# Spectral filter of batches 1 to 3: the sum of two products formed by an accumulating transfer from GpSimd

## The chip, the cores and the metric

The kernel runs on one core of one Trainium2 chip. The metric is device time in microseconds (us) for one execution; the time of a kernel is the median of several runs. The engines are named as in the profile: PE is TensorE's matmul, PEld its weight load, DVE is VectorE, ACT is ScalarE, POOL is GpSimd and SP is SyncE, whose queue issues the transfers of the kernel before. L12 is line 12 of the kernel.

## The reference

Three layers follow one another on a tensor of 4 batches, 3008 tokens and 256 features, all in float32. The first is a long convolution along the tokens, written as a filter in frequency space; the other two are wide feed-forward layers. The change touches the line `Y = X * F`.

```
X = np.fft.rfft(x, axis=1)
F = (filt_r + 1j * filt_i)[None, :, :]
Y = X * F
y = np.fft.irfft(Y, n=x.shape[1], axis=1)

h = x @ w_in                 # 256 -> 2048
x = square(maximum(h, 0)) @ w_out
g = x @ w_gate               # 256 -> 1536
out = (g * sigmoid(g) * (x @ w_val)) @ w_out2
```

## The kernel before

**Arithmetic.** A float32 matrix is split into a high part (ScalarE's copy to fp32r, `high`, L353) and a low part (VectorE's subtraction, `low`, L357). A product of two such pairs is three matmuls accumulated in PSUM (`product`, L365 to L367). So nearly every operand of TensorE passes through ScalarE and then through VectorE.

**The filter.** 3008 is 64 x 47. For each batch, step A (12 groups) transforms along the 64, and its result goes to the DRAM tensor `s1`. Then 16 pairs of rows `q` are worked on one at a time. Step B loads `bin` (from `s1`) and `fil` (the filter), 192 KB each, splits `bin` into `fhi` and `flo`, multiplies by a cosine and sine matrix into the PSUM bank `psB`, and applies the filter with `filtered` (L509). That function forms the product of both components with the real part (tile `t1`, L519), two products of the swapped components with the imaginary part and a sign (tile `t2`, L524, twice), and adds `t2` into `t1` (L536). All four are VectorE operations on 96 partitions. The trace writes `t` for both tiles. `fsplit` then splits the sum into a new `fhi` and `flo`, and step C, which is called one hook later, multiplies them into `psC`, copies the bank to `eb` and stores it into `s2`. Batch 0 is filtered ahead of everything by `first_ab`, with plain float32 matmuls; it also calls `filtered`. Batches 1 to 3 go through `stages_ab`, a few steps at a time, between the matmuls of the two feed-forward layers. They are 48 steps B and 48 steps C.

**The feed-forward layers.** The tokens are cut into column pairs (`WIDTH`, up to 2 x 512), and each layer goes through its weights in groups. Most of it uses a Strassen-Winograd scheme with seven products in place of eight (`slot1`, `slot2`): a PSUM bank (`pA`, `gA`, `vA`) is copied out by ScalarE (`snap`, L955), and then more products are accumulated on top of it, so the copy has to be done before TensorE goes on with that bank. The results are split (`ghi`, `glo`) and multiplied into the banks `acc`. The weights are decoded at the start (`decode`, VectorE L428 to L450), kept in DRAM and loaded group by group by SP.

**Order of the work.** All of it is recorded as steps in a list (`Plan`). `emit` goes through the list once, before the program is built. It keeps a clock for each of the five queues, and on the queue that is free first it takes the step that can begin first; among those within 0.12 us of one another it takes the one of lowest rank, which is mostly the order of declaration. So the order of every queue is fixed beforehand by assumed costs, and on the chip each engine executes its queue in that order and waits where an input is late. An SP transfer of `kb` KB is assumed to occupy the queue for 0.55 us, and its data to be there at

```
wire = max(wire, s.end) + s.kb / 370.0
s.end = max(s.end + 2.0 + s.kb / 230.0, wire + 1.8)
```

where `s.end` is the end of the issue and `wire` a clock for the DMA engines. Tiles come from small pools of buffers: `pool_f` has 12 for the filter's tiles, and a buffer is handed on in the order of declaration when its last user is done by the plan's clock.

Of the kernel before, what the change touches and what calls it, by code (L numbers as in the profile page):

```python
# [13 lines left out]
ALU = mybir.AluOpType  # L14
# [152 lines left out]
class Plan:  # L167
# [10 lines left out]
    def add(self, engine, cost, fn, r=(), w=(), rank=0, kb=0):  # L178
        s = Step()
        s.i, s.engine, s.cost, s.fn, s.kb = len(self.steps), engine, cost, fn, kb  # L180
        s.rank, s.after, s.end, s.start = len(self.steps) + rank + self.bias, [], None, None
        deps = set()
        for key in r:
            if key in self.last:
                deps.add(self.last[key])
        for key in w:
            if key in self.last:
                deps.add(self.last[key])
            deps.update(self.readers.get(key, ()))
        deps.discard(s.i)  # L190
        for key in w:
            self.last[key] = s.i
            self.readers[key] = []
        for key in r:
            if key not in w:
                self.readers.setdefault(key, []).append(s.i)
        tiles = []
        for key in list(r) + list(w):
            t = key[0] if isinstance(key, tuple) else key
            if isinstance(t, Tile) and t not in tiles:  # L200
                tiles.append(t)
                t.users += 1
        s.deps, s.tiles = deps, tiles
        self.steps.append(s)
        return s.i

    def emit(self):
        steps = self.steps
        waits = [len(s.deps) for s in steps]
        for s in steps:  # L210
            for d in s.deps:
                steps[d].after.append(s.i)
        engines = ["PE", "ACT", "DVE", "POOL", "SP"]
        now = {e: 0.0 for e in engines}
        wire = 0.0
        open_ = {e: [] for e in engines}
        base = {}
        frontier, entered = 0, 0
        done = 0

        def enter(s):
            at = 0.0
            for d in s.deps:
                o = steps[d]
                lag = self.CROSS[s.engine] if o.engine != s.engine else 0.03
                at = max(at, o.end + lag)
            base[s.i] = at
            open_[s.engine].append(s)

        def begin(s):  # L230

            at = base[s.i]
            for t in s.tiles:
                if t.slot is None:
                    b = t.buffers
                    if not b.loose and t.turn != b.taken:
                        return None
                    best = min((b.free[k] for k in t.among), default=None)
                    if best == float("inf"):
                        return None  # L240
                    at = max(at, best + 0.15)
            return at

        while done < len(steps):
            while entered < len(steps) and entered < frontier + self.WINDOW:
                if waits[entered] == 0:
                    enter(steps[entered])
                entered += 1
            pick, when = None, None
            for e in engines:  # L250
                best = None
                ready = []
                for s in open_[e]:
                    at = begin(s)
                    if at is not None:
                        ready.append((max(at, now[e]), s))
                if not ready:
                    continue
                first = min(a for a, _ in ready)
                for a, s in ready:  # L260
                    if a <= first + (0.12 if e != "SP" else 0.0) and (best is None or s.rank < best[1].rank):
                        best = (a, s)
                if pick is None or best[0] < when:
                    when, pick = best
            assert pick is not None, "no step can begin"
            s = pick
            open_[s.engine].remove(s)
            s.start = when
            now[s.engine] = when + s.cost
            s.end = when + s.cost  # L270
            if s.engine == "SP":
                wire = max(wire, s.end) + s.kb / 370.0
                s.end = max(s.end + 2.0 + s.kb / 230.0, wire + 1.8)
            for t in s.tiles:
                if t.slot is None:
                    b = t.buffers
                    k = min(t.among, key=lambda k: b.free[k])
                    t.slot = k
                    b.taken += 1
                    b.free[k] = float("inf")  # L280
                    t.t = b.pool.tile(t.shape, t.dtype, name=t.name, tag=b.tags[k], bufs=1)
            s.fn()
            for t in s.tiles:
                t.users -= 1
                t.end = max(t.end, s.end)
                if t.users == 0:
                    t.buffers.free[t.slot] = t.end
            done += 1
            for a in s.after:
                waits[a] -= 1  # L290
                if waits[a] == 0 and a < entered:
                    enter(steps[a])
            while frontier < len(steps) and steps[frontier].end is not None:
                frontier += 1
# [3 lines left out]
def fft_conv_moe_kernel(ctx, tc, x, filt, amat, cmat, sgn, w1, w2, wg, wv, wo, out):  # L298
    nc = tc.nc
# [6 lines left out]
    add = plan.add  # L306
# [35 lines left out]

    def dma(fn, r, w, kb, rank=0):
        add("SP", 0.55, fn, r, w, rank, kb)

    def act(fn, r, w, n=512, psum=False, rank=0):
        add("ACT", size(n, 0.54 if psum else 0.575), fn, r, w, rank)

    def dve(fn, r, w, n=512, cost=0.645, rank=0):
        add("DVE", size(n, cost), fn, r, w, rank)  # L350
# [26 lines left out]
    def narrow(pool, name, dtype=F32):  # L377
        return Tile(pool, [128, 512], dtype, name)
# [124 lines left out]
    def fsplit(t, n):  # L503
        hi, lo = narrow(pool_f, "fhi", F32R), narrow(pool_f, "flo", F32R)
        high(hi, t, lambda: hi.t[:n], lambda: t.t[:n])
        low(lo, t, hi, lambda: lo.t[:n], lambda: t.t[:n], lambda: hi.t[:n])
        return hi, lo

    def filtered(p, f, ff, q, t1, t2, engine):  # L509


        def pv():
            return p.t[:96].rearrange("p (c d) -> p c d", c=2)

        def cd(t):
            return t.t[:96].rearrange("p (c d) -> p c d", c=2)

        dve(
            lambda: nc.vector.tensor_tensor(cd(t1), pv(), ff()[:, 0:1, :].to_broadcast([96, 2, D]), op=ALU.mult),  # L519
            [p, f], [t1],  # L520
        )
        for c in range(2):
            dve(
                lambda c=c: nc.vector.scalar_tensor_tensor(  # L524
                    cd(t2)[:, c, :], pv()[:, 1 - c, :], sg[:, c, q:q + 1], ff()[:, 1, :], op0=ALU.mult, op1=ALU.mult
                ),
                [p, f, "sg"], [(t2, c)], cost=0.42,
            )
        if engine == "POOL":
            add(  # L530
                "POOL", 1.45, lambda: nc.gpsimd.tensor_tensor(t1.t[:96], t1.t[:96], t2.t[:96], op=ALU.add),
                [t1, (t2, 0), (t2, 1)], [t1],
            )
        else:
            dve(
                lambda: nc.vector.tensor_tensor(t1.t[:96], t1.t[:96], t2.t[:96], op=ALU.add),  # L536
                [t1, (t2, 0), (t2, 1)], [t1],
            )

    def stages_ab(b):  # L540
# [47 lines left out]
        def step_b(q):  # L588
            t, f = narrow(pool_f, "bin"), Tile(pool_f, [96, 2, D], F32, "fil")
            dma(  # L590
                lambda: nc.sync.dma_start(
                    t.t[:96].rearrange("p (c d) -> p c d", c=2),
                    v1[2 * q:2 * q + 2].rearrange("c p d -> p c d"),
                ),
                [("s1", b, g) for g in range(NG)], [t], 192, -60,
            )
            dma(lambda: nc.sync.dma_start(f.t, filt[:, q]), [], [f], 192, -60)
            hi, lo = fsplit(t, 96)
            special = load_special(0) if q == 0 else None
            p = bank("psB")  # L600
            slot_product(p, 0, q, hi, lo, special)
            t1, t2 = narrow(pool_f, "t1"), narrow(pool_f, "t2")
            filtered(p, f, lambda: f.t, q, t1, t2, "DVE")
            return fsplit(t1, 96)

        def step_c(q, hi2, lo2):
# [519 lines left out]
    for r, (layer, c) in enumerate(runs):  # L1126
# [60 lines left out]
        for g in range(G):  # L1187
            weights_of(g + 1)
            w, rows = ahead.pop(g)
# [48 lines left out]
```

## Time and profile before

| | us |
|---|---|
| median of 3 runs | 2271.76 |
| lowest and highest run | 2269.04, 2273.19 |
| span of the profiled execution | 2269.3 |
| TensorE busy in it | 2244.5 |
| VectorE busy | 1712.0 |
| ScalarE busy | 1381.1 |
| GpSimd busy | 0.2 |

The span goes from the first to the last instruction of one execution; that execution's own time is not given beside it, and the span lies within the three runs. Issuing a transfer does not count as busy time. Matmuls are pipelined and their ends are modelled, so a busy TensorE is one that has no gap; of two matmuls 0.39 us long the second starts 0.23 us after the first.

### The profile page before, as it was taken

To read this page: it belongs to the slowest core of one execution; us is meant where nothing else is said; L and a number is where in the kernel's file an instruction comes from. 1 tells how busy PE (TensorE), PEld (TensorE's weight loads), DVE (VectorE), ACT (ScalarE), POOL (GpSimd) and SP (SyncE) were. 2 spreads that over 40 slices of the span, in tenths; PEclk is the share of its full clock that TensorE was granted. 3 is DMA by queue.
4 is the path that set the end of the run, shared out by engine and by line. 5 is a ranking of instruction groups with operands and counts; after the bars stand their busy time and mean duration, and the time that the engine had idled before them with its cause. 6 is when DMAs were issued, how large, how long until landed. Compare 5 with 4: busy or idle time off the path is not lost.

```text
span 2269.3 us, 28911 instructions
## 1 busy us (share of the span) xinstructions
PE 2244.5 (99%) x10142; PEld 1855.8 (82%) x10142; DVE 1712.0 (75%) x2844; ACT 1381.1 (61%) x2464; POOL 0.2 (0%) x4
## 2 busy tenths in 40 slices
PE   6999999999999999999999999999999999999999
PEld 2688888888888887888888888888888888889889
DVE  3898898887678888667787787766776766767765
ACT  2788655565665656666566665655555655555655
POOL 0000000000000000000000000000000000000000
PEclk8999999999999999999999999999999999999999
DMA  9987768655765555656454555454454454445453
GB/s 287 361 284 258 251 238 278 214 187 194 241 206 164 165 175 187 209 200 218 158 164 141 188 184 167 166 179 163 153 172 131 156 180 160 160 153 169 153 190 135
DMA packets 201425, 439.03 MB, mean 193 GB/s; under 512 B 18080, under 2 KB 110496, under 8 KB 201280
## 3 DMA queue, kind: packets, MB, share of 16 engines
q1 hardware_dynamic: 201280, 437.18, 58.2%
q8 instruction: 80, 1.31, 0.2%
q14 instruction: 65, 0.53, 0.1%
HBM read 365.48 MB, written 71.63 MB: 193 GB/s over the span
## 4 chain that ended last, share of the span: by engine, by line
PE 96%; DMA 3%; ACT 0%; DVE 0%; issue 0%; SPq 0%; ACTq 0%
PE acc L365 13%; PE acc L367 13%; PE acc L366 13%; PE pA L365 3%; PE pA L366 3%; PE pA L367 3%; PE gA L365 3%; PE vA L365 3%; PE vA L367 3%; PE vA L366 3%; PE gA L366 2%; PE gA L367 2%; PE psx L790 2%; PE pC L365 2%; PE pC L367 2%; PE pC L366 2%
## 5 line engine op out<-in xcount | busy, mean ns | idle before, releaser
L367 PE MATMUL acc<-glo,ws 128*128 128x512 f32 (+2 forms) x1280 | 492.6, 385 | 0.0
L365 PE MATMUL acc<-ghi,ws 128*128 128x512 f32 (+2 forms) x1280 | 492.6, 385 | 0.0
L366 PE MATMUL acc<-ghi,ws 128*128 128x512 f32 (+2 forms) x1280 | 492.4, 385 | 0.0
L357 DVE TENSOR_TENSOR glo<-v,ghi 128x512 fp32r<-128x512 f32 (+2 forms) x438 | 291.8, 673 | 88.3 <-ACT ghi L353 83.9
L353 ACT CAST ghi<-v 128x512 fp32r<-128x512 f32 (+2 forms) x438 | 264.2, 610 | 125.0 <-DVE v L967 70.5
L365 PEld LDWEIGHTS acc<-ghi,ws 128*128 128x128 f32 x1280 | 240.2, 188 | 44.8
L367 PEld LDWEIGHTS acc<-glo,ws 128*128 128x128 f32 x1280 | 240.2, 188 | 44.8
L366 PEld LDWEIGHTS acc<-ghi,ws 128*128 128x128 f32 x1280 | 240.3, 188 | 44.5
L955 ACT COPY v<-pA 128x512 f32<-128x512 f32 (+2 forms) x240 | 138.3, 576 | 153.6 <-PE pA L367 149.4
L955 ACT COPY v<-vA 128x512 f32<-128x512 f32 (+2 forms) x198 | 114.2, 577 | 117.0 <-PE vA L367 112.3
L955 ACT COPY v<-gA 128x512 f32<-128x512 f32 (+2 forms) x198 | 114.1, 576 | 98.5 <-PE gA L367 95.2
L961 DVE TENSOR_TENSOR v<-vC,v 128x512 f32<-128x512 f32 (+2 forms) x132 | 89.6, 679 | 110.5 <-ACT v L955 109.6
L961 DVE TENSOR_TENSOR v<-pC,v 128x512 f32<-128x512 f32 (+2 forms) x160 | 108.3, 677 | 70.5 <-ACT v L955 40.7
L967 DVE SCALAR_TENSOR_TENSOR v<-v 128x512 f32<-128x512 f32 (+2 forms) x240 | 156.2, 672 | 2.4
L961 DVE TENSOR_TENSOR v<-gC,v 128x512 f32<-128x512 f32 (+2 forms) x132 | 89.5, 678 | 89.1 <-PE gC L367 74.3
L981 ACT ACTIVATE v<-v 128x512 f32<-128x512 f32 (+2 forms) x198 | 123.3, 623 | 50.5 <-DVE v L961 49.8
L987 DVE TENSOR_TENSOR v<-v 128x512 f32<-128x512 f32 (+2 forms) x198 | 133.0, 674 | 2.9
L357 DVE TENSOR_TENSOR glo<-r,ghi 128x512 fp32r<-128x512 f32 (+2 forms) x144 | 95.7, 676 | 4.9 <-ACT ghi L353 4.9
L353 ACT CAST ghi<-r 128x512 fp32r<-128x512 f32 (+2 forms) x144 | 88.4, 614 | 12.7 <-PE acc L366 9.2
L974 ACT ACTIVATE r<-pA 128x512 f32<-128x512 f32 (+2 forms) x80 | 47.0, 588 | 80.5 <-PE pA L367 79.9
L365 PE MATMUL pA<-z,wa 128*128 128x512 f32 (+2 forms) x240 | 93.0, 387 | 0.6 <-ACT v L955 0.6
L366 PE MATMUL pA<-z,wa 128*128 128x512 f32 (+2 forms) x240 | 92.3, 385 | 0.0
(224 smaller groups left out, 4735.7 us busy)
## 6 DMA issues: line engine op xcount, KB each, us to landing
wa<-dc SPq DMA_DIRECT2D x212, 512.0 KB, 3.5
ws<-ds SPq DMA_DIRECT2D x160, 512.0 KB, 4.4
wb<-db SPq DMA_DIRECT2D x212, 384.0 KB, 5.1
db<-po SPq DMA_DIRECT2D x20, 512.0 KB, 5.9
wa<-db SPq DMA_DIRECT2D x20, 512.0 KB, 4.7
dc<-po SPq DMA_DIRECT2D x20, 512.0 KB, 4.9
bin<-s SPq DMA_DIRECT2D x48, 192.0 KB, 5.6
fil<-in_filt SPq DMA_DIRECT2D x48, 192.0 KB, 5.5
```

The costliest lines, as they stand in the source:

```text
L353: act(lambda: nc.scalar.copy(fhi(), fsrc()), [src], [hi], n, psum, rank)
L357: lambda: nc.vector.tensor_tensor(flo(), fsrc(), fhi(), op=ALU.subtract), [src, hi], [lo], n, rank=rank
L365: nc.tensor.matmul(p, wl, mh, start=start, stop=False, skip_group_check=True)
L366: nc.tensor.matmul(p, wh, mh, start=False, stop=False, skip_group_check=True)
L367: nc.tensor.matmul(p, wh, ml, start=False, stop=stop, skip_group_check=True)
L790: nc.tensor.matmul(o.t[:, begin - n * w:end - n * w], x3[i // 5].t[:, i % 5, 128 * h:128 * h + 128], ai[:, first + begin - lo:first + end ...
L955: act(lambda: nc.scalar.copy(v.t[:, :w], p.t[:, :w]), [p], [v], w, True, URGENT)
L961: lambda: nc.vector.tensor_tensor(v.t[:, :w], p.t[:, :w], v.t[:, :w], op=ALU.add), [p, v], [v], w, rank=URGENT
L967: lambda: nc.vector.scalar_tensor_tensor(h.t[:, :w], h.t[:, :w], 0.0, h.t[:, :w], op0=ALU.max, op1=ALU.mult),
L974: act(lambda: nc.scalar.activation(h.t[:, :w], p.t[:, :w], AF.Relu), [p], [h], w, True, URGENT)
L981: lambda: nc.scalar.activation(t.t[:, :w], src.t[:, :w], AF.Silu), [src], [t], w, psum, URGENT if psum else 0
L987: lambda: nc.vector.tensor_tensor(g.t[:, :w], g.t[:, :w], src.t[:, :w], op=ALU.mult), [g, src], [g], w,
```

## The change

In the steps B of batches 1 to 3 the VectorE addition at L536 is left out. In its place GpSimd issues a transfer that reads `t2` (96 partitions x 2 KB, 192 KB) and adds it into `t1` in SBUF. Batch 0's 16 additions stay on VectorE. The planner gets assumptions for such a transfer: 1.0 us of GpSimd's queue, half of the SP transfer's rates, and the same constants.

```diff
@@ emit @@
+            if s.engine == "POOL":
+                wire = max(wire, s.end) + s.kb / 185.0
+                s.end = max(s.end + 2.0 + s.kb / 115.0, wire + 1.8)
             if s.engine == "SP":
                 wire = max(wire, s.end) + s.kb / 370.0
                 s.end = max(s.end + 2.0 + s.kb / 230.0, wire + 1.8)
@@ helpers @@
+    def add_dma(fo, fi, r, w, kb):
+        add("POOL", 1.0, lambda: nc.gpsimd.dma_start(fo(), fi(), accum_op=ALU.add), r, w, 0, kb)
@@ filtered @@
-        if engine == "POOL":
-            add(
-                "POOL", 1.45, lambda: nc.gpsimd.tensor_tensor(t1.t[:96], t1.t[:96], t2.t[:96], op=ALU.add),
-                [t1, (t2, 0), (t2, 1)], [t1],
-            )
+        if engine == "DMA":
+            add_dma(lambda: t1.t[:96], lambda: t2.t[:96], [t1, (t2, 0), (t2, 1)], [t1], 192)
         else:
             dve(
                 lambda: nc.vector.tensor_tensor(t1.t[:96], t1.t[:96], t2.t[:96], op=ALU.add),
@@ step_b @@
-            filtered(p, f, lambda: f.t, q, t1, t2, "DVE")
+            filtered(p, f, lambda: f.t, q, t1, t2, "DMA")
```

## Rows read from the trace of the kernel before

**Rows 1.** The page: busy time by engine, and the chain by engine.

```profile
PE 2244.5 (99%) x10142; PEld 1855.8 (82%) x10142; DVE 1712.0 (75%) x2844; ACT 1381.1 (61%) x2464; POOL 0.2 (0%) x4
...
PE 96%; DMA 3%; ACT 0%; DVE 0%; issue 0%; SPq 0%; ACTq 0%
```

**Rows 2.** Busy time by stretch: from:to, length, engines, granted clock, DMA share, GB/s.

```profile
0.00:56.70 56.70, 39.14 (x77) 15.43 (x78) 21.74 (x43) 14.16 (x24) 0.20 (x4) 0.83 0.95 287
...
1430.00:2269.00 839.00, 835.64 (x3891) 717.53 (x3889) 582.33 (x927) 487.24 (x871) 0.00 (x0) 1.00 0.49 161
...
198.00:1430.00 1232.00, 1229.79 (x5574) 1016.81 (x5573) 985.39 (x1659) 764.99 (x1360) 0.00 (x0) 1.00 0.60 199
```

**Rows 3.** VectorE's groups by line, 198 to 1430 us: the addition.

```profile
L536 DVE TENSOR_TENSOR t<-t,t 96x512 f32<-96x512 f32 x48 | 32.9, 686 | 1.3
```

**Rows 4.** TensorE's timeline: its waits; idle time and releaser in brackets.

```profile
524.53 0.47 PE L367 MATMUL psB<-flo,ch 96*96 96x512 f32 x1 [0.17 <-DVE flo L357]
895.11 0.50 PE L365 MATMUL gA<-z,wa 128*128 128x512 f32 x1 [0.95 <-ACT v L955]
1348.26 0.50 PE L365 MATMUL pA<-z,wa 128*128 128x512 f32 x1 [0.59 <-ACT v L955]
```

**Rows 5.** ScalarE's timeline: its five longest waits for a filter load.

```profile
522.01 0.62 ACT L353 CAST fhi<-bin 96x512 fp32r<-96x512 f32 x1 [2.94 <-DMA bin<-s]
...
538.61 0.62 ACT L353 CAST fhi<-bin 96x512 fp32r<-96x512 f32 x1 [2.24 <-DMA bin<-s]
555.47 0.62 ACT L353 CAST fhi<-xin 128x512 fp32r<-128x512 f32 x1 [2.50 <-DMA xin<-in_x]
...
893.96 0.62 ACT L353 CAST fhi<-bin 96x512 fp32r<-96x512 f32 x1 [1.99 <-DMA bin<-s]
...
1347.11 0.62 ACT L353 CAST fhi<-bin 96x512 fp32r<-96x512 f32 x1 [1.86 <-DMA bin<-s]
```

**Rows 6.** The chain that ended last, in order of time: start, length, what.

```profile
1340.08 6.95 DMA bin<-s
...
1347.63 0.58 ACT v L955
1348.26 0.50 PE pA L365
```

**Rows 7.** VectorE's timeline from the last of the 48 additions on.

```profile
1425.85 0.69 DVE L536 TENSOR_TENSOR t<-t,t 96x512 f32<-96x512 f32 x1
1426.45 0.68 DVE L357 TENSOR_TENSOR glo<-g,ghi 128x512 fp32r<-128x512 f32 x1
1427.06 0.68 DVE L987 TENSOR_TENSOR v<-v 128x512 f32<-128x512 f32 x1
1427.66 0.68 DVE L357 TENSOR_TENSOR flo<-t,fhi 96x512 fp32r<-96x512 f32 x1
...
1430.66 0.68 DVE L987 TENSOR_TENSOR v<-v 128x512 f32<-128x512 f32 x1
```

**Rows 8.** Landing of `bin`, and an issue group: KB each, median us to landing.

```profile
DMA to landing us min/median/max: 3.9/5.6/7.6
...
b<-s SPq DMA_DIRECT2D x8, 384.0 KB, 9.6
```

**Rows 9.** The waits: who waited for whom, us in total, times, longest.

```profile
ACT fhi L353 <- DMA bin<-s: 27.5, 27, 2.9
...
ACT fhi L353 <- DMA xin<-in_x: 12.7, 14, 2.5
```

**Rows 10.** Landing of step C's store out of SBUF, 192 KB.

```profile
DMA to landing us min/median/max: 2.0/3.7/7.0
```

**Rows 11.** SP's timeline and the chain: the next load, the next inverse product.

```profile
1437.64 0.38 SPq L773 DMA_DIRECT2D x<-s  x1
...
1511.31 0.89 PE psx L790 x8
```

**Rows 12.** Line 428 (weight decoding): ns min/median/max, first and last start.

```profile
L428 DVE TENSOR_SCALAR wa<-wa x34: 415/419/428, 30.4 to 284.6; 128x512 f32<-128x512 f32 x34
```

**Rows 13.** Tile `fhi`: step C's first matmul, first and last start.

```profile
L365 PE MATMUL psC<-fhi,cl x45: 392/398/473, 285.6 to 1432.9; 96*96 96x512 f32 x45
```

**Rows 14.** VectorE's timeline: the second and third of the 48 additions.

```profile
282.17 0.69 DVE L536 TENSOR_TENSOR t<-t,t 96x512 f32<-96x512 f32 x1
302.91 0.68 DVE L536 TENSOR_TENSOR t<-t,t 96x512 f32<-96x512 f32 x1
```

## The prediction

> **What bounds the kernel now.** I read the page's busy times first. TensorE is busy 2244.5 of 2269.3 us, VectorE 75%, ScalarE 61%, GpSimd does nothing, and the chain that ended last is 96% TensorE [rows 1]. The reader is to see that whatever is taken off VectorE is taken off an engine that already waits for others. The second view is the table of busy time by stretch [rows 2]. The 48 additions lie between 200 and 1426 us [rows 3], so I take 198 to 1430 us: TensorE is busy for 1229.79 of 1232.00 us there at a granted clock of 1.00 (its upper level, 2.4 GHz), VectorE for 985.39 us. Only 2.2 us of that stage can be won. In the first 56.7 us TensorE has 17.6 us of idle time, but there the filter is batch 0's, which keeps its VectorE addition; the last 839 us, with 3.4 us idle, hold no filter.
>
> The third view says what the 2.2 us are. TensorE's waits for other engines there are three: 0.17, 0.95 and 0.59 us [rows 4]. ScalarE's timeline shows what stood before each: a high-part cast `fhi<-bin` that waited 2.94, 1.99 or 1.86 us for the load of its input [rows 5]. ScalarE executes in order, so behind the cast stood a copy out of PSUM that a matmul needed. At 1347 us the chain is written out: a 6.95 us load, 0.58 us of ScalarE copy, then the matmul [rows 6]. This is the one way in which this stage loses time: **a transfer that lands later than the planner assumed blocks ScalarE's queue**. The change adds 48 such transfers ahead of 48 such casts.
>
> **The change, part by part.**
>
> *Removed from VectorE.* 48 additions at 686 ns, 32.9 us [rows 3]. On the path that sets the end they are worth 0: VectorE had 246 us idle in the stage, and no wait of TensorE's there names the addition. Uncovered it would cost 0.69 us for each step whose product waits. In the last step the split is done at 1428.34 us and TensorE first uses it at 1432.9 us [rows 7, 13], so 4.5 us of other matmuls lie between.
>
> *Added to GpSimd.* 48 issues on an idle queue [rows 1]. Each waits for the three VectorE products of its own step; nothing else is queued behind it on GpSimd. It is moved past no SP queue entry.
>
> *Added to the DMA engines.* 48 transfers that read 192 KB twice and write 192 KB. They move 48 x 0.576 = 28 MB against 245 MB in the stage (199 GB/s for 1232 us [rows 2]), with the DMA engines 60% busy. No TensorE wait in the stage is for a weight load, so I take 0.
>
> *Added latency, the disputed term.* The planner now assumes 1.0 + 2.0 + 192/115 = 4.67 us from the products to the sum (more where its modelled wire is backed up), and places the cast, the low part and the product after that. What counts is therefore not the latency but how far the true landing exceeds 4.67 us. For an SP transfer of 192 KB it assumes 0.55 + 2.0 + 192/230 = 3.38 us. The measured landing of `bin` is 3.9, 5.6 and 7.6 us (least, median, most) [rows 8], 2.2 us late at the median. What that lateness costs is measured: of the 72 loads of this kind (48 `bin`, 24 `xin`), 41 made ScalarE wait, 40.2 us in all [rows 9]; the planner had left slack before the others. TensorE lost 0.17 + 0.95 + 0.59 = 1.71 us, 0.024 us a load.
>
> The trace of before holds no accumulating transfer and none from GpSimd. From below: a 192 KB store out of SBUF landed in 2.0 us at the fastest, 3.7 at the median [rows 10]. From above: a 384 KB load, as many bytes as this one reads, took 9.6 us in the crowded opening [rows 8]. The nearest row is `bin`: the same 192 KB, destination, and stage. I take about 5.6 us, which is 0.9 us late, less than `bin` is; the second read and the descriptors written by GpSimd push up, a queue of its own without weight loads ahead of it pushes down. At `bin`'s price the 48 cost 48 x 0.024 = 1.1 us. At the lower end, at or before the plan, they cost 0.
>
> The price rises fast with lateness. The five longest waits in rows 5 (2.94, 2.50, 2.24, 1.99, 1.86 us, mean 2.31) cost 1.71 us together, 0.34 each, so the mean wait that TensorE survives is about 1.96 us. If every sum landed at 7.0 us, 2.3 us late and with no slack before the cast, the bill is 48 x 0.34 = 16.4 us. Beyond that all but the cover is lost: at 9.6 us, 4.9 us late, 48 x (4.93 - 1.96) = 143 us, the upper bound.
>
> The Trainium skill (DMA: Bandwidth & Descriptors, section Anatomy of one DMA — SWDGE (gpsimd) path) gives a transfer issued from GpSimd a fixed 2.0 us plus its bytes at 436 GB/s, an estimate of 2.45 us for 192 KB. By that the sums land ahead of the plan and the term is 0 in place of 1.1 us. The rows differ from it in direction: transfers of this size land at 3.7 and 5.6 us in this traffic, so I keep my own value.
>
> *Re-planning.* From the first changed step the greedy planner orders all five queues anew. It keeps TensorE full in its own account, so the order is worth 0 except for the three old stalls, which may vanish or recur: 0 to -1.7 us. The tail is safe too: after the last sum of batch 3 the next load of `s2` is issued at 1437.64 us, but the first inverse product that follows runs at 1511.31 us [rows 11], so 5 us of delay is covered 14 times over.
>
> *Sum.* 2269.3 (span of the profiled execution) + 0 (VectorE) + 1.1 (48 new waits) + 0 = 2270.4 us. The median of the runs, 2271.76, lies 2.46 us above that span, so 2272.9, rounded to **2273.0 us**. One profile shows no whole time beside its span, so I carry the 2.46 over.
>
> **Rivals.**
>
> *The sum lands well after the plan* (slower). Place: ScalarE's `fhi<-t` and VectorE's `flo<-t` in every step, with the PSUM copies behind them. For it: the three stalls above have exactly this shape. Against it: 38 of the 41 existing waits were absorbed. It decides from a mean loss of 0.1 us a step (4.5 us in all), between a wait of 0.9 and one of 2.3 us, so a landing of roughly 6 us without slack and 7.5 us with the 1.6 us that `bin` seems to have (2.2 us late, 0.56 us of wait per load). Landing at 7.0 us: 2272 + 16 = 2288 us; half of that bill 2280 us.
>
> *GpSimd is held up by VectorE while it writes descriptors* (slower, strongly). Place: VectorE's runs without a gap, such as the eight operations from 1426.45 to 1431.3 us [rows 7]. If GpSimd could not work during such a run, the sum would land up to 4.8 us later, near 10 us, and the bill would be 48 x (10.4 - 4.67 - 1.96) = 181 us at worst, some 60 us (2332) if one step in three meets such a run. For it: VectorE is busy 80% of the stage. Against it: no row, since GpSimd never worked beside VectorE here. The Trainium skill (SBUF — State Buffer, section Who interferes with whom) lets a transfer from GpSimd be held only by VectorE forms that use both ports, such as tensor_scalar, not by tensor_tensor. By that rule alone the rival would shrink to two steps: the tensor_scalar operations are the weight decoding's, and the last of that kind starts at 284.6 us, after two of the 48 additions [rows 12, 14]. No run yet shows it.
>
> *VectorE's relief is what counts* (faster). If the 32.9 us let the casts and copies behind VectorE come earlier, TensorE's 2.2 us in the stage could vanish: 2271.76 - 1.7 = 2270 us. It can't reach 0.2%, so it decides nothing unless the median falls low in its spread.
>
> *The transfer is hidden altogether*: landing before 4.67 us, 2271.8 us.
>
> **How the numbers follow.** About 0.2% (4.5 us) is what a measurement of this kernel can tell from no change; the three runs of before span 4.15 us. Chances: the forecast with its few small waits 0.40, hidden altogether or gained by up to 1.7 us 0.24 (of it 0.03 measured as faster than 0.2%), the late sum 0.26, GpSimd held up 0.10. The late sum and the held GpSimd give slower, less 0.01 for a bill under 4.5 us: 0.35. Same: 0.40 + 0.21 + 0.01 = 0.62. The range takes in the lowest run, less some of the old stalls (2269.0, less the half of 1.7: about 2268 us) and the late sum up to 16 us with the runs' spread of 2 us, 2290 us. It leaves out the held GpSimd, the worse part of the late sum, and 0.01 below: together under 0.2. For the forecast alone: 2269 to 2276 us.
>
> **What would show it.** Right: VectorE's busy time in the stage falls by about 33 us, TensorE idles 2 to 5 us between 198 and 1430 us, the transfers land at 5 to 6.5 us, and ScalarE's waits on them total 15 to 40 us, none over 3 us. Wrong in size: landing over 7 us and TensorE's waits on PSUM copies summing to more than 5 us. If descriptors are held up, GpSimd's issue is long exactly where VectorE has no gap. What would make the forecast wrong is one unknown: the landing time of an accumulating transfer from GpSimd in this traffic.

## The result and the profile after

The changed kernel takes 2287.5 us (median of 4 runs, 2282.9 to 2292.9) against 2271.0 us (4 runs, 2269.0 to 2273.2): a ratio of 1.0067, with a 95% interval of 1.0055 to 1.0079. It is slower by some 15 us. The profiled execution took 2286.5 us with a span of 2284.4, so 2.1 us lie outside its span. The line numbers after the change are 3 to 6 higher.

The page of the changed kernel, busy times and transfer queues (packets, MB, share of 16 engines); they answer to [rows 1]:

```profile
PE 2251.2 (99%) x10142; PEld 1854.2 (81%) x10142; DVE 1683.9 (74%) x2796; ACT 1377.6 (60%) x2464; POOL 38.9 (2%) x52
...
q1 hardware_dynamic: 201280, 437.18, 58.2%
q0 software_dynamic: 5376, 9.44, 2.8%
```

The change did what it says: VectorE has 48 instructions and 28 us less, GpSimd 48 instructions more, and a second transfer queue moved 9.44 MB. GpSimd's 38.9 us are almost all its 48 issues at 0.79 us; on this engine the page does count issuing a transfer as busy time.

The table by stretch, for the stage of the 48 sums, for two single landings, and for three neighbouring stretches around 400 us (columns as in [rows 2]):

```profile
198.00:1430.00 1232.00, 1222.72 (x5506) 1002.88 (x5505) 946.28 (x1593) 751.71 (x1343) 37.86 (x47) 1.00 0.66 205
831.50:838.00 6.50, 6.50 (x30) 5.14 (x28) 3.79 (x6) 2.09 (x5) 0.80 (x1) 1.00 0.88 253
1121.00:1124.70 3.70, 3.70 (x18) 3.05 (x17) 1.91 (x3) 2.23 (x4) 0.79 (x1) 1.00 0.56 90
396.40:398.30 1.90, 0.00 (x0) 0.00 (x0) 0.00 (x0) 0.65 (x2) 0.00 (x0) 1.00 0.94 327
398.30:401.70 3.40, 3.38 (x8) 2.44 (x9) 2.84 (x5) 2.02 (x4) 0.00 (x0) 0.50 1.01 405
401.70:405.00 3.30, 3.30 (x16) 2.83 (x16) 3.30 (x8) 1.52 (x3) 0.79 (x1) 0.99 0.24 72
```

In the same 1232 us TensorE does 5506 matmuls where [rows 2] have 5574. The 68 that are missing, at 1232/5574 = 0.221 us each, are 15.0 us: the whole difference of the spans (2284.4 - 2269.3 = 15.1). The displayed idle time (9.3 us against 2.2) is less, because a matmul that starts late hides part of its delay behind the modelled end of the one before it.

TensorE's waits in that stage are no longer three. Its timeline in the changed kernel, seven of fourteen such waits:

```profile
377.54 0.49 PE L371 MATMUL pA<-z,wa 128*128 128x480 f32 x1 [0.77 <-ACT v L958]
398.32 0.74 PE L371 MATMUL psB<-fhi,cl 96*96 96x512 f32 x1 [1.95 <-ACT fhi L359]
417.97 0.47 PE L371 MATMUL psB<-fhi,cl 96*96 96x512 f32 x1 [0.83 <-ACT fhi L359]
428.71 0.48 PE L371 MATMUL psC<-fhi,cl 96*96 96x512 f32 x1 [0.43 <-ACT fhi L359]
476.81 0.47 PE L371 MATMUL psC<-fhi,cl 96*96 96x512 f32 x1 [0.85 <-ACT fhi L359]
838.64 0.47 PE L371 MATMUL psC<-fhi,cl 96*96 96x512 f32 x1 [0.52 <-ACT fhi L359]
1407.30 0.50 PE L371 MATMUL pA<-z,wa 128*128 128x512 f32 x1 [0.20 <-ACT v L958]
```

Thirteen lie at 214 to 839 us and one at 1407 us: all but that one in batches 1 and 2. Two kinds are new, the first product of step B (`psB`) and that of step C (`psC`), each waiting directly for the cast that feeds it.

ScalarE's waits in the changed kernel (who waited for whom: us in total, times, longest), which answer to [rows 9]:

```profile
ACT fhi L359 <- DMA bin<-s: 42.2, 31, 3.3
ACT fhi L359 <- DMA t<-t: 41.9, 20, 4.9
...
ACT fhi L359 <- DMA xin<-in_x: 9.9, 11, 1.5
```

The sum brings 41.9 us of new waits, and the waits for `bin` grew from 27.5 to 42.2 us. The tile `t` in the changed kernel (ns min/median/max, first and last start) and the landing from the start of the issue:

```profile
L350 POOL DMA_DIRECT2D t<-t x48: 794/794/985, 200.7 to 1441.9; - x48
...
DMA to landing us min/median/max: 3.4/3.8/8.1
```

GpSimd begins 0.6 to 0.8 us after the last product, so I took the landings one by one from the trace, as time after that product: median 4.5 us, 31 of 48 at 4.1 to 4.9 us, 17 at 5.5 to 8.7 us, and nothing between 4.93 and 5.45. All 16 of batch 3 are among the 31. What separates the two groups is what SP had in flight: 1.4 us after their issue the 17 late sums had two to six SP transfers still under way beside them, the 31 early ones none or one (one of them two). VectorE does not separate them; it was busy for about three quarters of those 1.4 us in either group. Two of these stretches (columns as above):

```profile
507.10:508.50 1.40, 1.40 (x8) 1.17 (x7) 1.40 (x4) 0.54 (x1) 0.79 (x1) 1.00 0.04 6
762.40:763.80 1.40, 1.40 (x7) 1.14 (x7) 0.24 (x1) 1.40 (x3) 0.76 (x1) 1.00 0.79 252
```

The sum issued at 507.10 us beside a VectorE without a gap landed 3.4 us after its issue, the fastest of all, with the DMA engines 4% busy at its start. The one issued at 762.37 us took 6.2 us, with VectorE busy for 0.24 of the 1.40 us and the DMA engines 79% busy. One late landing in the timelines of SP, GpSimd, ScalarE and TensorE:

```profile
830.67 0.34 SPq L877 DMA_DIRECT2D wa<-dc  x1
832.03 0.34 SPq L892 DMA_DIRECT2D ws<-ds  x1
832.71 0.53 SPq L875 DMA_DIRECT2D wb<-db  x1
833.35 0.91 SPq L594 DMA_DIRECT2D bin<-s  x1
...
831.53 0.80 POOL L350 DMA_DIRECT2D t<-t  x1 [18.17 <-DVE v L970]
...
833.40 0.59 ACT L958 COPY v<-pA 128x512 f32<-128x512 f32 x1 [0.43 <-PE pA L373]
837.97 0.62 ACT L359 CAST fhi<-t 96x512 fp32r<-96x512 f32 x1 [3.99 <-DMA t<-t]
838.50 0.58 ACT L958 COPY v<-pA 128x512 f32<-128x512 f32 x1
```

Between 830.7 and 834.3 us SP issued 1.4 MB of weights and 0.4 MB of filter loads. The sum issued at 831.53 us landed 6.4 us later, ScalarE stood for 3.99 us, and step C's product at 838.64 us started 0.05 us after the cast's end. In the stretch table the DMA engines are 88% busy while this sum was in flight, and 56% while the one issued at 1121.01 us was, which landed in 3.6 us.

### The profile page after: what moved, and what is told of

It is laid out like the page before. It is cut to its first block, busy times and chain, and to the rows that moved or that the text cites. A ratio compares the mean times of both kernels' runs of the same rounds, so it can differ in the third digit from the quotient of the medians.

```text
span 2284.4 us, 29099 instructions
## 1 busy us (share of the span) xinstructions
PE 2251.2 (99%) x10142; PEld 1854.2 (81%) x10142; DVE 1683.9 (74%) x2796; ACT 1377.6 (60%) x2464; POOL 38.9 (2%) x52
## 3 DMA queue, kind: packets, MB, share of 16 engines
q0 software_dynamic: 5376, 9.44, 2.8%
## 4 chain that ended last, share of the span: by engine, by line
PE 62%; DMA 1%; ACT 0%; DVE 0%; issue 0%
PE acc L372 9%; PE acc L373 9%; PE acc L371 9%; PE pA L371 2%; PE pA L373 2%; PE pA L372 2%; PE vA L371 2%; PE vA L372 2%; PE vA L373 2%; PE gA L371 2%; PE gA L372 2%; PE gA L373 2%; PE psx L793 1%; PE pC L371 1%; PE pC L372 1%; PE pC L373 1%
```

## The experiments

TensorE's time lost in the stage, where I give it below, is worked out from the starts of consecutive matmuls between 198 and 1430 us: the time from one start to the next, less 1 us for 2400 columns and 13.5 ns, summed (for 512 columns that is 0.227 us, the median from start to start in the trace). It is 21.9 us before and 37.2 us after; most of the 21.9 is small change that every kernel here has. To say behind which transfer time was lost, I count the steps that lost over 0.1 us and put each down to the last wait of ScalarE for a transfer (over 0.3 us) in the 8 us before it. Before the change these steps come to 4.3 us: 3.1 behind `bin`, 1.2 behind `xin`. After it they come to 17.6 us: 8.3 behind the sum, 8.9 behind `bin`. This goes by the order of events and is an estimate.

| kernel | ratio to the kernel before | 95% interval |
|---|---|---|
| the change | 1.0067 | 1.0055 to 1.0079 |
| e1, its order, GpSimd adds | 1.0004 | 0.9995 to 1.0013 |
| e2, sum planned later | 1.0046 | 1.0032 to 1.0060 |
| e3, batch 3 only | 1.0005 | 0.9996 to 1.0013 |
| e4, transfer in the order of before | 1.0662 | 1.0646 to 1.0678 |
| e5, no sum at all | 1.0008 | 0.9999 to 1.0017 |
| e6, spare transfers, nobody waits | 1.0051 | 1.0038 to 1.0063 |
| e7, step C declared later | 1.0097 | 1.0082 to 1.0111 |
| e8, sum and `bin` planned later | 0.9988 | 0.9979 to 0.9997 |
| e9, e6 with `bin` planned later | 1.0007 | 0.9998 to 1.0017 |
| e10, before with `bin` planned later | 0.9990 | 0.9981 to 0.9999 |
| e11, e10 and `xin` too | 0.9991 | 0.9982 to 1.0000 |
| e12, e8 and `xin` too | 0.9981 | 0.9972 to 0.9990 |

**e1: the same order, another way to add.** Every queue but GpSimd's keeps the order of the changed kernel.

```diff
-        add("POOL", 1.0, lambda: nc.gpsimd.dma_start(fo(), fi(), accum_op=ALU.add), r, w, 0, kb)
+        add("POOL", 1.0, lambda: nc.gpsimd.tensor_tensor(fo(), fo(), fi(), op=ALU.add), r, w, 0, kb)
```

> Every queue has the order of the changed kernel; only the 48 sums are formed by a GpSimd addition in place of the transfer. Late-landing theory (20 of the 48 sums land 5.3 to 8.7 us after their products, where the plan has 4.67): the sums are now early, ScalarE waits for none of them, the stalls of step C's first products (6.3 us) go, those of step B's (4.8 us, behind late loads of bin) may stay: 2272 to 2279 us. Rival, order: the new order leaves no slack whatever forms the sum: 2284 to 2290 us. Rival, GpSimd held up by VectorE: the GpSimd addition itself is drawn out to several us and the time stays above 2284 us.

(The "20 of the 48" there are ScalarE's waits for the sum; landings of over 5.3 us are 17.) Measured: 2274.9 against 2273.7 us, no difference. GpSimd's own group in e1 (columns as in [rows 3]):

```profile
L350 POOL TENSOR_TENSOR t<-t,t 96x512 f32<-96x512 f32 x48 | 76.8, 1599 | 1356.2 <-DVE t L530 1016.3 <-PE pA L373 89.0 <-issue 52.1
```

The stage's row of the table by stretch in e1, with 59 matmuls more than after the change:

```profile
198.00:1430.00 1232.00, 1229.12 (x5565) 1014.13 (x5564) 973.29 (x1606) 762.04 (x1358) 74.64 (x47) 1.00 0.61 199
```

The addition takes 1.6 us, so the sum is early by the plan, and ScalarE waits for one of the 48 (1.3 us). The order that the planner made is harmless as long as inputs are there by its clock; the transfer itself costs the time. The rival of order falls, and so does that of a drawn-out addition. That GpSimd's transfers were not held up by VectorE is shown by the two stretches above and not by this run.

ScalarE's waits for `bin` in e1:

```profile
ACT fhi L359 <- DMA bin<-s: 36.4, 30, 3.6
```

Most of the growth from 27.5 to 42.2 us is therefore the order's, not the transfers', and 36.4 us of such waits cost next to nothing here. ScalarE's total says where to look, not what TensorE pays: by the steps over 0.1 us TensorE lost 5.0 us behind `bin` in e1 and 8.9 us after the change, in the same order.

**e2: the planner assumes the sum at 7.2 us.**

```diff
-                s.end = max(s.end + 2.0 + s.kb / 115.0, wire + 1.8)
+                s.end = max(s.end + 6.2, wire + 1.8)
```

> The transfer stays; the planner assumes that its sum is there 7.2 us after the products (1.0 + 6.2) and not 4.67. Late-landing theory: 43 of 48 landings are covered, ScalarE's waits for the sum fall from 41.9 us to under 10 us, and the time to 2270 to 2277 us. Rival, order: a longer chain in the plan leaves still less slack in batches 1 and 2: 2287 us or more.

Measured: 2282.9 us, between the theory and its rival. ScalarE's waits for the sum came down to 5 us, as expected, and yet two thirds of the loss stayed. TensorE's lost time in the stage fell only from 37.2 to 31.4 us. In e2 TensorE's and ScalarE's waits are

```profile
PE psB L371 <- ACT fhi L359: 4.1, 5, 2.5
...
ACT fhi L359 <- DMA bin<-s: 34.6, 20, 3.9
```

Late sums are a part of the cause and not the whole. What is left stands behind the loads of `bin`: by the steps over 0.1 us, 9.3 of 12.2 us, and 0.4 behind the sum. e2 has an order of its own, and no run has that order without the transfers, so what the order adds to this is not separated.

**e3: only batch 3's sums by transfer.**

```diff
-            filtered(p, f, lambda: f.t, q, t1, t2, "DMA")
+            filtered(p, f, lambda: f.t, q, t1, t2, "DMA" if b == 3 else "DVE")
```

> Only batch 3's 16 sums are formed by the transfer; batches 1 and 2 keep VectorE's addition. In the changed kernel all 16 of batch 3 landed within 4.93 us of their products and no ScalarE wait stood before them. Late-landing theory: no cost, 2270 to 2273 us. Rival, a fixed cost for each transfer (16 us over 48): 2276 us.

Measured: no difference (2275.1 against 2273.7 us; the kernel before itself took 0.7 us more here than the expected range). The rival's fixed cost, a third of 16 us, is 5.3 us and lies outside the interval, which ends at 3 us. Batch 3's 16 transfers show no cost by their traffic either.

**e4: the transfer in the order of before.** The step is recorded with VectorE's cost and on VectorE's clock, but GpSimd issues it.

```diff
-        add("POOL", 1.0, lambda: nc.gpsimd.dma_start(fo(), fi(), accum_op=ALU.add), r, w, 0, kb)
+        dve(lambda: nc.gpsimd.dma_start(fo(), fi(), accum_op=ALU.add), r, w)
```

> The transfer is issued, but every queue keeps the order of the kernel before, in which the cast of the sum stands about 0.85 us behind the products. Late-landing theory: with landings 4.1 to 8.7 us after the products ScalarE waits 3.4 to 7 us 48 times, some 210 us in all, and TensorE, which survives about 2 us of each, loses some 100 us: 2340 to 2420 us. Rival, order: the order of before is the good one: 2271 to 2280 us.

Measured: 2423.0 us, 149 us more and 3 us above the expected range. The waits in e4:

```profile
ACT fhi L359 <- DMA t<-t: 208.4, 47, 9.7
...
PE psC L371 <- ACT fhi L359: 48.7, 23, 5.6
```

The 210 us of waits came as expected. Each cost TensorE 149/48 = 3.1 us out of 4.4 us of mean wait, more than the 2.5 us that a cover of about 2 us gives. But the mean granted clock of that execution was 0.974 against 0.995 before, and 0.021 of 2426 us is some 50 us: up to a third of the 149 us may be the lower clock after long stalls, and not the waits themselves.

**e5: VectorE's relief alone.** The kernel before without the 48 additions.

```diff
-            filtered(p, f, lambda: f.t, q, t1, t2, "DVE")
+            filtered(p, f, lambda: f.t, q, t1, t2, None)
...
-        else:
+        elif engine == "DVE":
```

> The kernel before without the 48 additions and with nothing in their place (the sums are left out, the first product is passed on): VectorE's relief alone, 32.9 us of its time. My step that the relief is worth nothing: 2269 to 2276 us, the same as before within 0.2%. Rival, relief: VectorE's freed time reaches TensorE and the time falls by over 4.5 us.

Measured: no difference (2274.8 against 2272.7 us). Even a sum that costs nothing would gain nothing, in the order that the planner then makes.

**e6: the traffic alone.** VectorE adds as before; then a transfer of the same size adds `t1` into `t2`.

```diff
-                wire = max(wire, s.end) + s.kb / 185.0
-                s.end = max(s.end + 2.0 + s.kb / 115.0, wire + 1.8)
+                s.end = s.end + 3.7
...
-            add_dma(lambda: t1.t[:96], lambda: t2.t[:96], [t1, (t2, 0), (t2, 1)], [t1], 192)
+            dve(
+                lambda: nc.vector.tensor_tensor(t1.t[:96], t1.t[:96], t2.t[:96], op=ALU.add),
+                [t1, (t2, 0), (t2, 1)], [t1],
+            )
+            add_dma(lambda: t2.t[:96], lambda: t1.t[:96], [t1], [(t2, 0), (t2, 1)], 192)
```

The planner gives such a transfer 3.7 us and leaves its clock for the DMA engines alone. So the order, compared by the names of the tiles, comes out as that of the kernel before, but for 12 of TensorE's 10142 places, 7 of ScalarE's 2464 and 19 of SP's 1108.

> The kernel before with VectorE's additions, and behind each of the 48 a transfer of the same size and kind that adds the sum into the second product's tile, which nobody reads afterwards. Traffic and GpSimd's issues alone, no engine waits for them. Late-landing theory, in which only the wait for the sum costs: within 3 us of the kernel before. Rival, traffic: the added transfers delay the loads of bin and the weights by themselves: 5 us or more.

My theory fell here: 2283.9 against 2272.7 us, 11 us for 9.44 MB that nobody waits for, in nearly the order of the kernel before. ScalarE's waits in e6:

```profile
ACT fhi L358 <- DMA bin<-s: 47.1, 32, 3.5
```

The landing of `bin` from its issue in e6, in the view of that tile:

```profile
DMA to landing us min/median/max: 2.6/6.0/9.0
```

Against [rows 8] the median of `bin` rose from 5.6 to 6.0 us and the longest from 7.6 to 9.0, and ScalarE's waits for it from 27.5 [rows 9] to 47.1 us. The traffic makes loads late that were already later than the plan. By the steps over 0.1 us TensorE lost 9.8 us behind `bin`, where it lost 3.1 before, and 3.2 us behind two more casts of `bin`, whose wait the profile puts down to a store `s<-eb`. The changed kernel and e1, which share one order, say the same of the landing: the median of `bin` is 5.9 us with the transfers and 5.6 without.

**e7: step C declared one step B later.**

```diff
+        held = None
         for q in range(NQ):
             pair = step_b(q)
             yield
-            step_c(q, *pair)
+            if held is not None:
+                step_c(q - 1, *held)
+            held = pair
             yield
+        step_c(NQ - 1, *held)
```

> The changed kernel, with step C of each row pair declared one step B later, so that its product has a whole step more before it is due; the casts of the sum stay where the planner expects the sum. Theory that TensorE's direct waits for step C's operands (6.3 us) are the largest share of the loss: 2279 to 2283 us. Rival, ScalarE's queue: the casts still block the PSUM copies behind them, nothing is gained: 2285 us or more. If the added slack also relieves step B's products: 2275 us or less.

Measured: 2295.1 us, worse than the change. TensorE's waits for step C's operands are gone, but ScalarE's are all there, and the copies behind them pay:

```profile
ACT fhi L359 <- DMA t<-t: 41.8, 22, 4.7
...
PE pA L371 <- ACT v L962: 6.0, 6, 2.4
```

Declaring the product later moves TensorE's use, not the cast: the planner takes a cast as soon as it believes its input to be there. What has to be mended is the belief.

**e8: both landings planned for.** As e2, and the load of `bin` is assumed 2.5 us later (5.9 us from its issue). `plan.late` is set around that one transfer.

```diff
-                s.end = max(s.end + 2.0 + s.kb / 230.0, wire + 1.8)
+                s.end = max(s.end + 2.0 + s.kb / 230.0, wire + 1.8) + s.late
...
+            plan.late = 2.5
             dma(
                 lambda: nc.sync.dma_start(
                     t.t[:96].rearrange("p (c d) -> p c d", c=2),
...
+            plan.late = 0.0
```

> As e2_later_assumed, and the planner also assumes that the load of bin lands 2.5 us later than it did (5.9 us from its issue). In e2 the casts of the sum waited no more, and the loss left (9.5 us in the stage) stood behind loads of bin with a product placed right behind them. Theory, the late loads in a chain without slack are what is left: 2271 to 2277 us. Rival, a longer chain itself costs: 2282 us or more.

Measured: 2270.1 against 2272.7 us. The whole loss is gone, with the same 48 transfers. ScalarE's waits in e8:

```profile
ACT fhi L359 <- DMA t<-t: 5.5, 9, 1.2
```

The stage's row in e8:

```profile
198.00:1430.00 1232.00, 1231.36 (x5588) 1019.28 (x5587) 963.00 (x1615) 761.73 (x1364) 38.59 (x48) 1.00 0.66 207
```

**e9: the traffic alone, with `bin` planned later** (the edits of e6 and of e8's `late` together).

> As e6_spare_transfer (VectorE's sums and 48 added transfers that nobody waits for, 11 us slower), but the planner assumes the loads of bin 2.5 us later. Theory that the added traffic costs only through loads of bin that land later than planned (ScalarE's waits on them rose from 28.9 to 53.3 us): under 5 us of ScalarE's waits on bin are left and the time is 2268 to 2273 us. Rival, the traffic slows the weight loads or something else: 2278 us or more.

Measured: 2274.1 against 2272.4 us. Of the 11 us the planning of `bin` takes back most, but not all that was expected: ScalarE's waits for `bin` are 8.0 us, not under 5, and the time is 1 us above the expected range. (The expectation's 28.9 and 53.3 us count the casts put down to `s<-eb` too; the rows give 28.7 and 53.3.) Against its control e10 (0.9990) the ratio is 0.17% higher, about 4 us. The two intervals touch, but with one kernel before for both, e9's median of 11 runs is 4.3 us above that of e10. Part of the rest can be seen in e9's trace, which is of an execution of 2278.3 us, 4 us above the median. By the steps over 0.1 us TensorE lost 5.1 us behind `bin` there and 3.4 behind `xin` (0.1 and 1.6 in e10). The largest single loss is 4.2 us from 395 to 401 us, partly at the lower clock: a cast of `bin` had waited 3.0 us, and then VectorE, which had the low part of `bin` to form, stood for a load `sum` that no plan had moved:

```profile
396.98 0.49 DVE L482 TENSOR_TENSOR sum<-sum 128x128 f32<-128x128 f32 x2 [3.96 <-DMA sum<-dw]
...
398.13 0.74 PE L372 MATMUL psB<-flo,ch 96*96 96x512 f32 x1 [2.09 <-DVE flo L362]
```

So the traffic reaches other loads as well. Whether that is the whole rest stays open, and so does why e8, with the same traffic, shows none of it: e8 lacks VectorE's 48 additions and has another order, and no run separates these.

**e10 to e12: what the planning gives without and with the transfer.** e10 is the kernel before with e8's edit on `bin`; e11 has the same 2.5 us on `xin` as well; e12 is e8 with `xin`.

> The kernel before with VectorE's sums; only the assumption on bin is 2.5 us later. It is the control for e8_both_later, which has the transfer and the same assumption. If the transfer by itself is worth nothing once both landings are planned for, this comes out as e8 within 3 us: 2267 to 2272 us. Rival, the relief of VectorE showed in e8: 2272 us or more.

> As e10, and the loads of xin are assumed 2.5 us later as well; the last stalls in e8 (1.5 us) stood behind xin. Expected within 2 us of e10, 2266 to 2271 us, the lowest that planning alone can give, since TensorE lost 3.5 us to stalls in the stage before. Rival, a longer chain costs: over 2273 us.

> The transfer with all three landings (sum, bin, xin) assumed later: 2266 to 2271 us, as e11. If the transfer beats VectorE's addition once it is planned for, this is below e11 by 2 us or more; if its traffic costs even then, above it by as much.

Measured: 2269.8, 2270.2 and 2268.2 us against 2272.4 us. The intervals of e8, e10, e11 and e12 overlap: once the landings are planned for, the transfer is worth as much as VectorE's addition to within 0.1%. e12's median is 2.0 us below that of e11, just the 2 us that its expectation named for a gain by the transfer; the two differ in order too, so such a gain is neither shown nor excluded. e12 is the fastest kernel here, 0.19% below the kernel before; its stage has no TensorE wait left:

```profile
198.00:1430.00 1232.00, 1232.00 (x5594) 1021.39 (x5593) 964.25 (x1618) 763.01 (x1366) 38.59 (x48) 1.00 0.66 207
```

## Why the prediction was right or wrong, step by step

The time lies in the stated range, but the likeliest case was not the one that came. The forecast was 2273 us and no change; the measured 2287.5 us is the first rival's, "the sum lands well after the plan", with its 2288 us. That the two agree so closely is luck: the 2288 us come from all 48 sums landing at 7.0 us at 0.34 us each, while 17 came late and a part of the loss is another's. Of the signs named for being right, none but VectorE's relief came: TensorE's displayed idle time was 9.3 us (2 to 5 expected), the landings lay outside 5 to 6.5 us for the most part, and ScalarE's waits for the sum were 41.9 us, up to 4.9 (15 to 40, none over 3).

**What bounds the kernel: right.** TensorE does, late transfers ahead of ScalarE's casts are how it loses time, and VectorE's relief is worth nothing. e5 shows the last.

**"At `bin`'s price the 48 cost 48 x 0.024 = 1.1 us": this step failed.** In the same order, with the sum early, the time is that of the kernel before (e1); with the transfer it is 15 us more. That is 0.3 us a transfer, thirteen times the price. Three things were wrong in it.

First, the landing. The typical landing, 4.5 us after the products, was earlier than my 5.6 us. But a median decides nothing where only the landings later than the planned 4.67 us can cost: 17 of 48 came at 5.5 to 8.7 us. I had argued that a queue of its own, without weight loads ahead, would push the landing down. The runs show that the queue is its own and the DMA engines are not: the first packet of a sum began 1.4 us after its issue in the 31 early sums, and 1.5 to 4.4 us after it in 16 of the 17 late ones, which stood among SP's transfers.

Second, the cover, which is the time from the end of the sum's cast to step C's first product. I took 4.5 us of other matmuls from the last step of batch 3 [rows 7, 13]. In the kernel before the median was indeed 5.5 us in batch 3, but 2.5 us in batches 1 and 2. In the order of the change with the sum in time (e1) it is 1.7 us in batch 3 and 2.1 us in the others: in batch 3 the planner used up most of the slack. In the changed kernel late casts left a median of 1.1 us in batches 1 and 2, and under 0.1 us in 8 of 32 steps. So "the order is worth 0" is true (e1), but the same order has little room for a late input. That all but one of TensorE's new waits lie in batches 1 and 2, and that e3 is free, is due to the landings and not to the cover: all 17 late ones are in batches 1 and 2.

Third, the price. It was an average over loads, most of which the planner had scheduled with slack, and it was read from displayed idle time, 1.71 us. By the starts of the matmuls TensorE lost 4.3 us behind the same loads, 0.06 us a load and not 0.024. e4 shows the price without slack: 3.1 us, the clock's share included.

**"No TensorE wait in the stage is for a weight load, so I take 0": this step failed too.** The 48 transfers delay the loads of `bin`, which had no room left. I looked at the weight loads, which are issued a group ahead, and not at the transfers on the narrow path that I had just named. (The profile counts 9.44 MB for the 48, where I had 28; how it counts their second read no run shows.) e6 shows this effect alone at 0.51%, in nearly the order of before. e2, where the sum's waits are gone, leaves 0.46% of the 0.67%, in an order of its own. These do not give the shares within the changed kernel. There the steps over 0.1 us put 8.3 us behind the sum, and behind `bin` 8.9 us against 5.0 in e1, which has its order and no added traffic: by this estimate the wait for the sum is the larger part of what e1 does not pay, and the traffic's delay of `bin` the smaller. That both are at work is shown, their shares are not. e8 takes both away by planning and not by moving a byte less; e9 leaves some 4 us of the traffic's share only partly explained where VectorE adds as well.

**The held GpSimd: refuted.** GpSimd's issue took 794 ns at the median and 985 ns at the most, beside a VectorE that was busy for 946 of 1232 us, and late landings went with SP's transfers and not with VectorE's work. By the rule that I cited from the Trainium skill (SBUF — State Buffer, section Who interferes with whom), VectorE's two-input additions should not hold it, and the trace agrees. (The last tensor_scalar of the weight decoding starts at 286.69 us, at L440, and not at 284.6; that is still ahead of the third sum [rows 14].) The other rule, from the Trainium skill (DMA: Bandwidth & Descriptors, section Anatomy of one DMA — SWDGE (gpsimd) path), gave an estimate of 2.45 us; the fastest of the 48 landed 3.4 us after its issue and the slowest 8.1, so here the measurement decides.

## What to carry to other kernels

In an order fixed beforehand by assumed costs, an in-order engine waits for every input that is later than the assumption, and the planner can spend slack that it believes it has: after adding an asynchronous step, compare its landings one by one with the assumed time, and look at the late third, not at the median. Added transfers cost first where a load already lands later than planned, even when nobody waits for the added ones; look for those loads in the waits of the engine that they block, but take the price from the engine that sets the time. Before moving work off an engine, leave that work out once (e5): if nothing gets faster, there is little for any way of moving it to win.

## What the runs showed of the hardware that was not expected

TensorE stood for 1.95 us before 398.32 us in the changed kernel. Its granted clock was then 0.50 (1.2 GHz, the lower level) for 3.40 us, in which 8 matmuls started, and 16 started in the 3.30 us after it: a stall of 1.95 us cost some 1.7 us more (8 matmuls fewer, at about 0.21 us). It isn't so each time: in e6 TensorE stood for 2.02 us before 907.47 us and the granted clock stayed at 1.00.

GpSimd's addition of 96 x 512 float32 took 1599 ns, against 686 ns on VectorE [rows 3].
